# Threshold attention and FFN: a new order of the first blocks, weight sums on TensorE, thresholds on ScalarE

## The chip, the cores and the metric

One core of a Trainium2 chip. The metric is the device time of one execution in microseconds (us), as a median of several runs. A profile is one execution recorded on the chip; its engines are PE (TensorE), PEld (its weight loads), DVE (VectorE), ACT (ScalarE), POOL (GpSimd) and SP (the queue that issues DMAs).

## The reference

```python
# q, k, v: (8 batches, 8 heads, 576 rows, 64); w_in (512, 2048) and w_out (2048, 512) in float64
scores = (q @ k.T) / 8
scores = where(scores >= max(scores) - tau, scores, -1e9)
attn   = exp(scores - max(scores));  attn /= attn.sum() + 1e-9
x      = (attn @ v)  -> (4608 tokens, 512)
out    = maximum(x @ w_in, 0) ** 2 @ w_out
```

## The kernel before

A *block* is 128 rows of queries of a pair of heads; there are 160 of them (the fifth of a pair has 64 rows for each head). A *slot* finishes block n and begins block n+1. A *piece* is 256 tokens of the feed-forward part, which is multiplied with Strassen-like products and so needs sums of weight quarters. The weights come as float64; each of 32 chunks is turned to float32 by a pipeline of *conversion steps* over ScalarE, GpSimd and VectorE:

```python
def weights_step():                 # step m; 36 steps in all
    convert3(m - 4)                 # GpSimd: integer add into w_in / w_out, frees r
    convert1(m - 2)                 # ScalarE: a = |hi|; GpSimd: clip a; ScalarE: r   (2 buffers of r)
    convert2(m - 3)                 # VectorE: shift a, merge into the raw words
    ...                             # fetch the next chunk; make sums due when their chunks are there

def combine_in(n):                  # sums of w_in, on GpSimd, 128x1024 each
    yield plus(e, s1, a21, a22)
    yield minus(e, a21, a11, a21)
    yield minus(e, s2, s1, a11)
    yield minus(e, s4, a12, s2)     # (w_out likewise, half on VectorE)
```

The attention of a block, and the order of a slot:

```python
def softmax(i, t, sc):              # sc: scores in PSUM, two heads
    # VectorE: nmx = -max of each head; thr = -nmx - tau
    # ScalarE: w = exp(sc + nmx), one instruction for each head
    yield
    # VectorE: w = (sc >= thr) * w, with its sum in sm ("the last pass")
    # VectorE: sm += 1e-9; reciprocal;   GpSimd: w *= sm ("normalise")

def slot(n, steps):
    if turns(n): turn(slots[n][0] + 1)             # transpose the next q and k
    begin(n + 1, lambda: weights_due(0))           # scores, softmax; a step between exp and last pass
    values_after(n - 1)                            # attn @ v, copies of x on ScalarE
    ...
    transposes(*slots[n])                          # PE transposes w; ScalarE copies wR, wT, wT
    for k in range(1, steps): weights_due(k)       # a second step, from slot 7 on
```

In the first slots (while weights are converted) every engine runs its instructions in this program order, or nearly so (the trace shows a few of VectorE's swapped from block 8 on). PSUM holds the results of this kernel's matmuls, in banks of 512 float32 columns. In slots 0 to 6 there are two PSUM buffers for scores and two other banks; from slot 7 on one buffer for scores and four other banks. In later slots only PE's order is fixed, and the order on the other engines is the framework's.

## Time and profile before

1628.1 us (1627.2 to 1630.9).

| | before |
|---|---|
| PE busy | 1515.6 us of a span of 1626.5 (93%) |
| DVE, ACT, POOL busy | 867, 586, 592 us |
| row maxima of block 8 / 20 / 26 begin at | 76 / 193 / 245 us |
| PE idle from 245 us on | 37.4 us of 1381.5 |
| PE busy and mean granted clock, 12 to 245 us | 166.5 us of 233, clock 0.81 |

The important reading is by time. Until 245 us PE is idle over a quarter of the time and runs at a lowered clock; after it the kernel is one dense stretch of PE work. So there are two questions for any change: when does the dense stretch start, and how much PE work is left then? The start of a block's row maxima (VectorE's reduction, nmx) is a good mark, as every block has one. Its lines are shown in the prediction.

### The profile page before, as it was taken

The page shows a single profiled execution, that of the slowest core. Times are in us where ns is not written, and L with a number is a line of the kernel's source. Part 1 is how long each engine was busy: PE and PEld are TensorE (multiplying, and loading weights), DVE is VectorE, ACT ScalarE, POOL GpSimd, SP SyncE. Part 2 cuts the span into 40 slices and gives each one's busy share as a digit, 9 for nine tenths or more (in the row PEclk, how much of TensorE's full clock was granted, in tenths as well). Part 3 has the DMA queues.
Part 4 walks back from the last instruction along what each step waited for, and adds up shares of the span by engine and source line. Part 5 has one row for each costly group of instructions (what it writes and reads, how often), then busy time and mean ns, then how long its engine had stood idle before and what let it go on. Part 6 is the DMA issues. An engine that isn't in the chain of part 4 may idle for free.

```text
span 1626.5 us, 25919 instructions
## 1 busy us (share of the span) xinstructions
PE 1515.6 (93%) x10084; PEld 1216.1 (75%) x10084; DVE 867.0 (53%) x1792; ACT 585.7 (36%) x1273; POOL 592.1 (36%) x630
## 2 busy tenths in 40 slices
PE   5676789999999999999999999999999999999998
PEld 2344567778787778778788887878777787878987
DVE  4678974645555564646444455555646464553222
ACT  3545633434343333433333243333433333431100
POOL 2488662332424232334141424232423333233131
PEclk8877889999999999999999999999999999999999
DMA  4334401111010101010101010101011101000000
GB/s 126 109 108 131 128 22 35 23 29 30 23 36 14 31 23 35 23 36 16 35 8 30 21 36 10 34 23 35 23 36 23 35 16 29 15 1 14 14 14 14
DMA packets 107914, 58.69 MB, mean 36 GB/s; under 512 B 89873, under 2 KB 99089, under 8 KB 107793
## 3 DMA queue, kind: packets, MB, share of 16 engines
q1 hardware_dynamic: 107792, 57.04, 12.9%
q8 instruction: 80, 1.31, 0.3%
q14 instruction: 42, 0.34, 0.1%
HBM read 47.58 MB, written 9.44 MB: 35 GB/s over the span
## 4 chain that ended last, share of the span: by engine, by line
PE 77%; DVE 12%; ACT 6%; POOL 3%; issue 2%; SPq 0%; DMA 0%; ACTq 0%; DVEq 0%; POOLq 0%
PE ph L482 27%; PE po L556 25%; PE sc L326 11%; PE pwT L397 6%; DVE nmx L340 5%; ACT w L350 4%; PE pv L428 3%; PE pqk L287 2%; PE pwR L386 2%; DVE s L170 1%; DVE w L355 1%; ACT x L436 1%; PE pv L423 1%; DVE g L491 1%; POOL w L369 1%
## 5 line engine op out<-in xcount | busy, mean ns | idle before, releaser
L369 POOL TENSOR_SCALAR w<-w,sm 128x576 f32<-128x576 f32 (+1 forms) x320 | 237.4, 752 | 643.9 <-DVE sm L360 638.4
L340 DVE TENSOR_REDUCE nmx<-sc 128x1 f32<-128x576 f32 x288 | 206.1, 752 | 206.7 <-PE sc L326 188.9
L355 DVE SCALAR_TENSOR_TENSOR w<-sc,thr,w 128x576 f32<-128x576 f32 x288 | 225.0, 815 | 132.7 <-ACT w L350 130.2
L350 ACT ACTIVATE w<-sc,nmx 128x576 f32<-128x576 f32 x288 | 199.8, 741 | 259.0 <-DVE nmx L340 258.9
L556 PE MATMUL po<-w_out,g 128*128 128x256 f32 x1152 | 261.5, 382 | 11.2 <-ACT x L436 6.1
L556 PEld LDWEIGHTS po<-w_out,g 128*128 128x128 f32 x1152 | 216.1, 191 | 41.0 <-ACT x L436 7.3
L326 PE MATMUL sc<-kT,qT 64*128 64x64 f32 (+3 forms) x1248 | 215.6, 461 | 24.5 <-DVE w L355 24.4
L482 PE MATMUL ph<-x,w_in 128*128 128x128 f32 x1728 | 209.5, 278 | 2.1 <-ACT x L436 2.1
L326 PEld LDWEIGHTS sc<-kT,qT 64*128 64x128 f32 (+1 forms) x1248 | 105.5, 181 | 137.1 <-issue 124.6
L482 PEld LDWEIGHTS ph<-x,w_in 128*128 128x128 f32 x1728 | 203.2, 195 | 3.2 <-ACT x L436 2.3
L397 PE MATMUL pwT<-ident,w 128*128 128x128 f32 x1024 | 146.3, 281 | 44.2 <-ACT x L436 25.7
L397 PEld LDWEIGHTS pwT<-ident,w 128*128 128x128 f32 x1024 | 117.1, 143 | 56.8 <-ACT x L436 37.1
L398 ACT COPY wT<-pwT 128x512 f32<-128x512 f32 x256 | 145.2, 594 | 24.6 <-PE pwT L397 20.8
L482 PE MATMUL ph<-xt,s_in 128*128 128x128 f32 x1152 | 142.4, 278 | 4.3 <-POOL s_in L167 3.3
L428 PE MATMUL pv<-wT,va 128*64 128x320 f32 (+1 forms) x1024 | 141.8, 420 | 0.0
L482 PEld LDWEIGHTS ph<-xt,s_in 128*128 128x128 f32 x1152 | 136.0, 194 | 6.2 <-POOL s_in L167 4.9
L170 DVE TENSOR_TENSOR u<-ph,u 128x512 f32<-128x512 f32 x108 | 74.6, 690 | 112.4 <-PE ph L482 84.2
L556 PE MATMUL po<-t_out,g 128*128 128x256 f32 x576 | 132.2, 379 | 0.0
L428 PEld LDWEIGHTS pv<-wT,va 128*64 128x64 f32 x1024 | 69.4, 140 | 66.5 <-issue 29.9
L556 PEld LDWEIGHTS po<-t_out,g 128*128 128x128 f32 x576 | 107.7, 190 | 13.5
L493 POOL TENSOR_TENSOR g<-p 128x512 f32<-128x512 f32 x36 | 37.8, 1049 | 156.4 <-ACT p L510 156.4
L482 PE MATMUL ph<-x,s_in 128*128 128x128 f32 x576 | 71.9, 279 | 0.0
(79 smaller groups left out, 1623.6 us busy)
## 6 DMA issues: line engine op xcount, KB each, us to landing
kn<-in_k_dram SPq DMA_DIRECT2D x72, 128.0 KB, 3.1
va<-in_v_dram SPq DMA_DIRECT2D x36, 256.0 KB, 2.8
out_dram<-o SPq DMA_DIRECT2D x36, 256.0 KB, 2.0
raw<-in_moe_w_in_dram SPq DMA_DIRECT2D x16, 512.0 KB, 4.0
raw<-in_moe_w_out_dram SPq DMA_DIRECT2D x16, 512.0 KB, 3.8
qn<-in_q_dram SPq DMA_DIRECT2D x56, 128.0 KB, 2.4
rn<-in_q_dram SPq DMA_DIRECT2D x36, 32.0 KB, 2.4
rn<-in_k_dram SPq DMA_DIRECT2D x36, 32.0 KB, 2.7
```

The costliest lines, as they stand in the source:

```text
L170: e.tensor_tensor(out=out, in0=x, in1=y, op=ALU.add)
L326: nc.tensor.matmul(to, qT[rows, ds(t * P, m)], kT[rows, ds(k0, n)], start=True, stop=True)
L340: nc.vector.tensor_reduce(out=nmx[:, j : j + 1], in_=sc[:, ds(at[j], S)], axis=AXIS.X, op=ALU.max, negate=True)
L350: nc.scalar.activation(out=w[:, ts(j, S)], in_=sc[:, ds(at[j], S)], func=AF.Exp, bias=nmx[:, j : j + 1], scale=1.0)
L355: nc.vector.scalar_tensor_tensor(out=w[:, ts(j, S)], in0=sc[:, ds(at[j], S)], scalar=thr[:, j : j + 1], in1=w[:, ts(j, S)], op0=ALU.is_ge, ...
L369: nc.gpsimd.tensor_scalar(out=out, in0=w, scalar1=r, scalar2=1.0, op0=ALU.mult, op1=ALU.mult)
L397: nc.tensor.transpose(pt[:, c, :], w[:, ds(j * (S + REST) + c * P, P)], ident[:, :])
L398: nc.scalar.copy(wT[:, j, :, at], pt[:, :, :])
L428: nc.tensor.matmul(pv[rows, :], va[:, j, c, :], wT[:, j, c, 0:n], start=False, stop=(c == FULL - 1), skip_group_check=True,)
L482: nc.tensor.matmul(to[:, j, :], a, b, start=(not more and j == 0 and c == 0), stop=(c == 1), skip_group_check=True,)
L493: e.tensor_tensor(out=to, in0=c[:, :, :], in1=c[:, :, :], op=ALU.mult)
L556: nc.tensor.matmul(to[:, :], a[:, f, :], b[:, f, :], start=(not more and f == 0), stop=(f == KF - 1), skip_group_check=True,)
```

## The change

Its intent: in the first slots, let PE have its PSUM banks back sooner by copying transposes before the next block's exponentials are through; move the sums from GpSimd to TensorE, which is idle there; relieve VectorE of two small instructions a block.

```diff
+    def combine(out, x, y, sign):            # one PSUM bank, 128x512
+        nc.tensor.matmul(pt, ident, x, start=True, stop=False)
+        nc.tensor.matmul(pt, ident if sign > 0 else nident, y, start=False, stop=True)
+        evicted["n"] += 1                    # then copied out, in turn on ScalarE and VectorE
...                                           # combine_in: 8 sums, twice; combine_out: 16 sums
-        nc.vector.tensor_scalar(out=thr, in0=nmx, scalar1=-1.0, scalar2=tau_p, op0=mult, op1=subtract)
+        nc.scalar.activation(out=thr, in_=nmx, func=AF.Identity, bias=tau_n, scale=-1.0)
+        yield
         for j in range(nj):
             nc.scalar.activation(out=w[j], in_=sc[j], func=AF.Exp, bias=nmx[j], scale=1.0)
-        yield
+            yield
...
-        nc.vector.tensor_scalar(out=sm, in0=sm, scalar1=1e-9, scalar2=None, op0=ALU.add)
+        nc.scalar.activation(out=sm, in_=sm, func=AF.Identity, bias=eps, scale=1.0)
...                                           # transposes() yields after each wT copy
     def slot(n, steps, n_sums):
-            begin(n + 1, lambda: weights_due(0))
+        job = begin(n + 1)                   # scores, row maxima, threshold
...
-        transposes(*slots[n])
-        for k in range(1, steps):
-            weights_due(k)
+        for _ in transposes(*slots[n]):
+            next(job, None)                  # wR, wT, exp, wT, exp
+        for _ in job:
+            pass                             # last pass, epsilon, reciprocal, normalise
+        for k in range(steps):
+            weights_step()
+        for k in range(n_sums):
+            sums_step()                      # 3 a slot
...
-            slot(n, 1)
+            slot(n, 2 - n % 2, 3)            # slots 0 to 6; the early stage ends at slot 25, not 23
```

More of the change, by code (lines that the diff above doesn't have):

```diff
@@ L92 @@
     )
-    tau_p = const.tile([P, 1], FP32, name="tau_p")
-    nc.vector.tensor_scalar(out=tau_p[:, :], in0=tau_c[:, :], scalar1=0.0, scalar2=None, op0=ALU.max)
+    tau_n = const.tile([P, 1], FP32, name="tau_n")
+    nc.vector.tensor_scalar(
+        out=tau_n[:, :], in0=tau_c[:, :], scalar1=0.0, scalar2=-1.0, op0=ALU.max, op1=ALU.mult
+    )
+    eps = const.tile([P, 1], FP32, name="eps")
+    nc.gpsimd.memset(eps[:, :], 1e-9)
+    nident = const.tile([P, P], FP32, name="nident")
+    nc.gpsimd.tensor_scalar(
+        out=nident[:, :], in0=ident[:, :], scalar1=-1.0, scalar2=1.0, op0=ALU.mult, op1=ALU.mult
+    )
     vdiag = [const.tile([P, P], FP32, name=f"vdiag{i}") for i in range(2)]
@@ L170, in plus @@
         e.tensor_tensor(out=out, in0=x, in1=y, op=ALU.add)
+    evicted = {"n": 0}
+    def combine(out, x, y, sign):
+        pt = bank([P, WC], "comb")
+        nc.tensor.matmul(pt[:, :], ident[:, :], x, start=True, stop=False)
+        nc.tensor.matmul(pt[:, :], ident[:, :] if sign > 0 else nident[:, :], y, start=False, stop=True)
+        if len(out.shape) == 3:
+            pt = pt.rearrange("p (f o) -> p f o", f=out.shape[1])
+        evicted["n"] += 1
+        if evicted["n"] % 2:
+            nc.scalar.copy(out, pt)
+        else:
+            nc.vector.tensor_copy(out=out, in_=pt)
@@ L172, in combine_in @@
     def combine_in(n):
-        e = nc.gpsimd
         first, second = ts(n, WC), ds(HF + n * WC, WC)
-        a11, a12 = w_in[:, 0:2, first], w_in[:, 2:4, first]
-        a21, a22 = w_in[:, 0:2, second], w_in[:, 2:4, second]
-        s1, s2, s4 = (s_in[:, m, :, first] for m in range(3))
-        yield plus(e, s1, a21, a22)
-        yield minus(e, a21, a11, a21)
-        yield minus(e, s2, s1, a11)
-        yield minus(e, s4, a12, s2)
-    def combine_out(k):
-        first, second = ds(k, 4), ds(KF + k, 4)
-        b11, b12 = w_out[:, first, 0:HD], w_out[:, first, HD:DM]
-        b21, b22 = w_out[:, second, 0:HD], w_out[:, second, HD:DM]
-        t1, t2, t4 = (t_out[0][:, m, first, :] for m in range(3))
-        minus(nc.vector, t1, b12, b11)
-        yield minus(nc.gpsimd, b12, b22, b12)
-        minus(nc.vector, t2, b22, t1)
-        yield minus(nc.gpsimd, t4, b21, t2)
+        for what in (0, 3, 1, 2):
+            for c in range(2):
+                a11, a12 = w_in[:, c, first], w_in[:, 2 + c, first]
+                a21, a22 = w_in[:, c, second], w_in[:, 2 + c, second]
+                s1, s2, s4 = (s_in[:, m, c, first] for m in range(3))
+                out, x, y, sign = ((s1, a21, a22, 1), (s2, s1, a11, -1), (s4, a12, s2, -1), (a21, a11, a21, -1))[what]
+                combine(out, x, y, sign)
+                yield
@@ new lines, in combine_out @@
+    def combine_out():
+        for what in range(4):
+            for k in range(0, KF, 2):
+                first, second = slice(k, k + 2), slice(KF + k, KF + k + 2)
+                b11, b12 = w_out[:, first, 0:HD], w_out[:, first, HD:DM]
+                b21, b22 = w_out[:, second, 0:HD], w_out[:, second, HD:DM]
+                t1, t2, t4 = (t_out[0][:, m, first, :] for m in range(3))
+                out, x, y = ((t1, b12, b11), (b12, b22, b12), (t2, b22, t1), (t4, b21, t2))[what]
+                combine(out, x, y, -1)
+                yield
@@ L202 @@
     at_step = {"n": 0}
-    sums_due = deque()
+    sums_due, sums_made = deque(), set()
     def weights_step():
@@ L214, in weights_step @@
         if m - 4 in (n_in // 2 - 1, n_in - 1):
-            sums_due.append(combine_in((m - 4) // (n_in // 2)))
+            n = (m - 4) // (n_in // 2)
+            sums_due.append((n, combine_in(n)))
         if m == len(chunks) + 3:
@@ L219, in weights_step @@
             t_out.append(late.tile([P, 3, KF, HD], FP32, name="t_out"))
-            sums_due.extend(combine_out(k) for k in range(0, KF, 4))
+            sums_due.append((2, combine_out()))
     def sums_step():
         while sums_due:
-            if next(sums_due[0], 0) is None:
+            if next(sums_due[0][1], 0) is None:
                 return
-            sums_due.popleft()
+            sums_made.add(sums_due.popleft()[0])
     def weights_until(n):
-        while at_step["n"] < n:
-            weights_step()
-        while at_step["n"] == n and sums_due:
-            sums_step()
+        while n not in sums_made:
+            if sums_due:
+                sums_step()
+            else:
+                weights_step()
     N_STEPS = len(chunks) + 4
@@ L344, in softmax @@
         thr = sb.tile([P, 2], FP32, tag="thr", bufs=3, name="thr")
-        nc.vector.tensor_scalar(
-            out=thr[:, 0:nj], in0=nmx[:, 0:nj], scalar1=-1.0, scalar2=tau_p[:, :], op0=ALU.mult, op1=ALU.subtract
+        nc.scalar.activation(
+            out=thr[:, 0:nj], in_=nmx[:, 0:nj], func=AF.Identity, bias=tau_n[:, :], scale=-1.0
         )
         w = sb.tile([P, 2 * S], FP32, tag="w", bufs=2, name="w")
+        yield
         for j in range(nj):
@@ L352, in softmax @@
             )
-        yield
+            yield
         for j in range(nj):
@@ L358, in softmax @@
             )
-        nc.vector.tensor_scalar(out=sm[:, 0:nj], in0=sm[:, 0:nj], scalar1=1e-9, scalar2=None, op0=ALU.add)
+        nc.scalar.activation(out=sm[:, 0:nj], in_=sm[:, 0:nj], func=AF.Identity, bias=eps[:, :], scale=1.0)
         nc.vector.reciprocal(out=sm[:, 0:nj], in_=sm[:, 0:nj])
@@ L398, in transposes @@
                 nc.scalar.copy(wT[:, j, :, at], pt[:, :, :])
+                yield
         else:
@@ L404, in transposes @@
                 nc.scalar.copy(wT[:, j, :, at], pt[:, :, ds(j * REST, REST)])
+            yield
     def values(i, t0, t1):
@@ L497, in feed_forward @@
         for n in range(2):
-            weights_until(4 + (n + 1) * n_in // 2)
+            weights_until(n)
             X = pm()
@@ L540, in feed_forward @@
         minus(nc.vector, g21, g11, g21)
-        weights_until(N_STEPS)
+        weights_until(2)
         t1, t2, t4 = (t_out[0][:, m, :, :] for m in range(3))
@@ L625, with begin @@
     n_first, n_batch = NP * HALF, NP * NB
-    def begin(n, between=lambda: None):
+    def begin(n):
         i, t = slots[n]
@@ L630, in begin @@
         next(job)
-        between()
-        next(job, None)
+        return job
     def values_after(n):
@@ L651, in turns, with slot @@
         return i + 1 < len(visits) and t == max(visits[i][2] - 2, visits[i][1])
-    def slot(n, steps):
-        def weights_due(k):
-            if k < steps:
-                if at_step["n"] < N_STEPS:
-                    weights_step()
-                sums_step()
+    def slot(n, steps, n_sums):
         if turns(n):
             turn(slots[n][0] + 1)
-        if n + 1 < len(slots):
-            begin(n + 1, lambda: weights_due(0))
+        job = begin(n + 1) if n + 1 < len(slots) else iter(())
         with_values = values_after(n - 1)
@@ L671, in slot @@
             load_v(i + 2)
-        transposes(*slots[n])
-        for k in range(1, steps):
-            weights_due(k)
+        for _ in transposes(*slots[n]):
[3 more added lines that the diff above has]
+        for k in range(steps):
+            if at_step["n"] < N_STEPS:
+                weights_step()
+        for k in range(n_sums):
+            sums_step()
         return with_values
@@ L686 @@
         turn(0)
-        begin(0)
+        for _ in begin(0):
+            pass
         for n in range(n_first - 1):
-            slot(n, 1)
+            slot(n, 2 - n % 2, 3)
     with ExitStack() as stack:
@@ L693 @@
         late = 0.0
-        n_early = n_first - 1 + (N_STEPS + 4 - n_first) // 2
+        n_early = n_first - 1 + (N_STEPS - at_step["n"] + 1) // 2 + 6
         for n in range(n_first - 1, len(slots)):
@@ L698 @@
             with tc.manual_schedule(engines={ET.PE, ET.DVE, ET.Activation, ET.Pool} if early_on else {ET.PE}):
-                with_values = slot(n, 2 if early_on else 1)
+                with_values = slot(n, 2 if early_on else 1, 3)
                 if n < n_first:
```

## The prediction

> **What bounds the kernel now.** I first read the busy time by stretches (columns: stretch, length, busy us and number of instructions of PE, PEld, DVE, ACT and POOL, granted TensorE clock, DMA share, GB/s).
>
> ```profile
> 12.00:70.00 58.00, 38.20 (x162) 21.25 (x162) 32.74 (x78) 27.29 (x58) 21.62 (x31) 0.76 0.38 105
> 70.00:218.00 148.00, 104.84 (x619) 74.67 (x618) 125.41 (x205) 77.12 (x162) 116.06 (x107) 0.82 0.40 112
> 218.00:245.00 27.00, 23.50 (x121) 17.42 (x120) 15.13 (x30) 9.27 (x22) 15.90 (x13) 0.84 0.10 23
> 245.00:1626.50 1381.50, 1344.11 (x9177) 1100.54 (x9173) 692.62 (x1479) 469.89 (x1027) 436.78 (x469) 1.00 0.09 24
> ```
>
> From 245 us on, PE is 97% busy at full clock and every other engine has room: only PE work counts there. What the change can win lies in the first 245 us, where PE is busy 172 us at a clock of 0.76 to 1.0. Busy time times clock is 29.0 + 86.0 + 19.7 = 135 us between 12 and 245, so an estimate of the slack is 233 - 135 = 98 us.
>
> Then the waits of the first 260 us (us in total, times, longest):
>
> ```profile
> ACT w L350 <- DVE nmx L340: 50.1, 18, 8.6
> ACT r L144 <- POOL w_out L164: 24.7, 9, 5.7
> ACT r L144 <- POOL w_in L164: 20.2, 6, 5.6
> PE sc L326 <- DVE w L355: 20.2, 7, 5.3
> PE pwT L397 <- ACT wR L388: 13.9, 4, 3.7
> PE pwT L397 <- ACT x L436: 11.9, 6, 5.7
> ```
>
> PE waits for ScalarE's copies of transposes, which stand behind the next block's exponentials, and for VectorE's last pass over the scores. ScalarE itself waits 45 us in the weight conversion (r), for GpSimd to free one of two r buffers. This wait I expect to decide the matter. The timeline of one two-step block (start, length) shows how it hangs together:
>
> ```profile
> 174.10 0.17 DVE L360 RECIPROCAL sm<-sm 128x2 f32<-128x2 f32 x1
> ...
> 174.43 1.96 POOL L369 TENSOR_SCALAR w<-w,sm 128x576 f32<-128x576 f32 x2 [1.29 <-DVE sm L360]
> 176.36 1.29 POOL L164 TENSOR_TENSOR w_out<-raw,r 128x512 int32<-128x512 int32 x1
> 177.75 0.61 POOL L140 TENSOR_SCALAR a<-a 128x512 f32<-128x512 f32 x1
> 178.32 1.30 POOL L164 TENSOR_TENSOR w_out<-raw,r 128x512 int32<-128x512 int32 x1
> ...
> 177.69 0.68 ACT L144 ACTIVATE r<-raw 128x512 int32<-128x512 uint32 x1 [3.15 <-POOL w_out L164]
> 178.27 1.36 ACT L350 ACTIVATE w<-sc,nmx 128x576 f32<-128x576 f32 x2
> ```
>
> Reciprocal, two normalisations, one integer add on GpSimd, r on ScalarE, then the exponentials: in these early blocks each engine runs in program order, so this is one loop. By the starts of the row maxima (nmx), blocks 1 to 7 begin at 18.4 to 69.7 us, 8.6 us apart (6.7 to 7.0 without a turn of the next q and k, 9.6 to 10 with one). Block 8 begins at 76.4, block 22 at 209.6: 9.5 us each, although two of them stalled on GpSimd's weight sums. Block 26 begins at 245.3, with one piece's hidden half and 48 output matmul instructions done (48 x 216 ns = 10.4 us; 24 of them took 5.18 us in the chain).
>
> **What the Trainium skill says.** "ScalarE: Activation LUTs", What ACT_TABLE_LOAD costs: an ACTIVATE with a per-partition bias costs about 280 ns + 0.833 ns per element. The trace agrees: 0.76 us for 576 elements against 0.741 measured; so a 128x2 threshold is an estimated 0.28 us. "GPSIMD Engine Reference", 8. Key points: it shares SBUF interfaces with VectorE, and contends with its two-port modes. The trace agrees: VectorE's shift (L152) has a median of 0.43 us and takes 1.45 beside GpSimd at 178.46. "PSUM — Partial Sum Buffer", The four PSUM rules: one matmul output is at most one bank, 512 fp32 columns; so each new sum of 128x512 takes one whole bank until it is copied out. No run here shows that yet. "TensorE: Matmul & The Clock Gate", What's actually happening: PE's clock falls when idle and is released by work; agreed, 0.76 to 0.84 before 245 us and 1.00 after.
>
> **The change, part by part.**
>
> *Sums on TensorE.* Removed: 8 GpSimd adds of w_in at 2.35 us (18.8), 4 of w_out (2.36 and 2.87 us, together 10.4), and 4 on VectorE (6.4). Added: 32 sums of 128x512, two fp32 matmuls each. An fp32 matmul is two instructions; a 256-column one takes 216 ns in a dense run, so 512 columns twice is 0.86 us, and 64 matmuls are 55 us of PE at full clock. Also 16 copies on ScalarE (0.59, 9.5 us) and 16 on VectorE (0.69, 11 us). PE is the bound after 245 us, so these 55 us are free only as far as they fill the 98 us of slack. GpSimd's stalls go: row maxima of blocks 10 and 11 lie 18.2 us apart, some 8 us over a usual block; PE waited 104.8 us into the run for s_in.
>
> *Thresholds and epsilon on ScalarE.* VectorE loses two small instructions of 0.17 to 0.23 us a block (0.47 and 0.38 early, under contention); ScalarE gets two of 0.28, one ahead of the exponentials and one between VectorE's last pass and the reciprocal, with two crossings of engines.
>
> *Copies between exponentials.* In program order ScalarE now does threshold, wR copy 0.27, wT 0.59, exp, wT, exp. PE gets its banks earlier, so in the first stage scores need no longer wait for the exponentials. But VectorE's last pass (0.81 each) now waits for later exponentials, and **the conversion steps move behind all of it**: before, the first step lay between the exponentials and that pass, so VectorE converted while ScalarE ran exp.
>
> One two-step block by these durations, from the start of the row maxima: 1.43 both maxima; threshold to 1.8; wR 2.05; wT 2.6; exp 3.3; wT 3.9; exp 4.6; last pass to 5.6; epsilon 5.9; reciprocal 6.1; normalised 7.65; first integer add on GpSimd 8.95; its clip a 9.55; second add 10.85. ScalarE's r: 9.65 and 11.5. VectorE's second conversion needs that clip: 9.7 to 10.9. Only then come the next maxima: **10.9 us a block**. The same loop before is reciprocal 174.1 to reciprocal 182.34: 8.2 us. A one-step block that is followed by a turn: r ends at 9.65, qT 10.15, last transpose 10.4, scores 11.6, rest scores 12.1, next maxima: 12.1 us.
>
> First stage: slots 0 to 6 take 2, 1, 2, 1, 2, 1, 2 steps: 4 x 10.9 + 3 x 12.1 = 79.9, so block 8 begins at 18.4 + 79.9 = 98 us (76.4 before), with 13 of 36 steps done instead of 9. Then 12 slots of two steps: 12 x 10.9 = 131; less 8 for four blocks of a single head half; plus about 18 for hidden-layer adds on VectorE (0.69), turns, and PE waiting for banks in five slots with sums, whose copies stand at the end of ScalarE's and VectorE's order: block 20 at 239. Then 13 sums (22 us) and six slots of about 5.4 us of PE work: 4.0 for attention (1515.6 us of PE busy on the page, less 18 pieces at the code's 48.9 us, over 160 blocks) and 1.44 of hidden layer by the code's quota; at 97%, block 26 at 295. Against 245.3 that is +50, and PE has 10.4 us of output work less behind it: **+60**, so 1689.
>
> **Rivals.**
> *Slack is filled.* If PE ran dense from 12 us on it would need 135 + 55 = 190 us: about 43 us won, 1586. For it: PE's waits for copies and for scores are just those attacked, and GpSimd's bursts vanish. Against: VectorE is already busy 125 of 148 us, the sums use up over half the slack, and the loop above does not run through PE. Half of this (loops of 8 us, sums hidden in gaps) would be 1610 to 1630.
> *The loop is shorter than worked out.* If a buffer comes free earlier, or VectorE without contention (0.43 for 1.45 us) speeds the steps, 1.5 us off each of 19 blocks is -28: 1661.
> *A new wait on the steady path.* Two more ScalarE instructions and crossings lie before scores can be reused in all 160 blocks. For: PE waits there 20.2 us early. Against: after 245 us a block takes some 10 us of PE work, and scores to last pass takes about 7. At most +10 us.
>
> **Range and chances.** The loop's arithmetic gives 1689. Errors of 1 to 2 us in 19 to 25 blocks are 30 to 40 us. I choose a middle of 1682, since the parameters (steps, three sums a slot, six more slots) look tuned and may save something that I do not see. 1640 to 1725 should hold it 8 times in 10. Two per cent is 32.6 us, so slower begins at 1661.5: 0.66. Within 2%: 0.29. Faster would need nearly all the slack: 0.05.
>
> **What would show it.** PE busy about 50 us more in all; from some 300 us on the same 97% at full clock. Row maxima 10 to 12 us apart in blocks 1 to 20, with r still waiting for GpSimd, now behind the normalisation; block 8 near 98 us, block 26 near 295. GpSimd less busy early by 29 us. Fewer PE waits for wR and wT. I am wrong if blocks keep to 8 or 9 us with the steps at their end, or if sums sit in gaps with no later start of the dense part; then the time is about as before or less. If blocks are short but the dense part is less full than 96%, the third rival was underrated.

## The result and the profile after

1706.2 us (1704.2 to 1706.5, 4 runs): slower, ratio 1.047 (95% interval 1.046 to 1.049). A ratio here is the mean time of one kernel's runs over that of the other's in the same rounds, so not quite the ratio of the medians quoted. Executions over 1.5% slower than the fastest of the same kernel are left out of the means.

The stretches of the changed kernel (columns as in the prediction), with the boundary at 327 us, where its block 26 begins:

```profile
12.00:100.00 88.00, 44.90 (x168) 24.38 (x170) 39.11 (x71) 35.00 (x79) 28.43 (x36) 0.67 0.31 88
100.00:250.00 150.00, 111.20 (x504) 66.47 (x501) 81.15 (x133) 71.73 (x157) 68.65 (x73) 0.81 0.32 94
250.00:327.00 77.00, 68.45 (x324) 39.79 (x324) 35.67 (x66) 29.66 (x73) 19.84 (x23) 0.94 0.09 20
327.00:1704.70 1377.70, 1348.13 (x9209) 1106.76 (x9205) 628.12 (x1212) 532.63 (x1297) 448.07 (x475) 1.00 0.09 24
```

Block 26 begins at 327 us instead of 245, 82 us later. All engines are less busy than before in the early stretch: VectorE 120 of the 238 us from 12 to 250, where it was busy 173 of the 233 from 12 to 245. So nothing is overloaded; the engines wait for each other. Busy time times clock up to 327 us is 30.1 + 90.1 + 64.3 = 185 us: 50 us more PE work done than in the kernel before at its block 26, and 130 us of slack where there were 98. By then 8 output matmul instructions were done instead of 48, which leaves some 9 us more for later. And the dense stretch has 29.6 us of PE idle where it had 37.4. 82 + 9 - 8 = 83, against a difference of spans of 78; the account is good to some 5 us, since the busy time of matmuls is modelled.

The waits of the first 300 us of the changed kernel:

```profile
POOL w L397 <- DVE sm L388: 159.3, 23, 10.6
DVE w L383 <- ACT w L378: 69.7, 22, 6.7
...
ACT sm L387 <- DVE w L383: 31.6, 22, 1.7
ACT r L152 <- POOL w_in L172: 30.6, 15, 3.0
ACT r L152 <- POOL w_out L172: 25.3, 14, 3.0
...
PE pwR L414 <- POOL w L397: 17.1, 7, 4.8
...
PE sc L353 <- DVE w L383: 12.8, 5, 5.9
```

And one line of the same view of before, for its first 260 us:

```profile
DVE w L355 <- ACT w L350: 8.5, 14, 1.4
```

PE's waits for the last pass did go down (20.2 to 12.8 us), but VectorE now waits 70 us for exponentials (8.5 before), and r still waits for GpSimd, 56 us instead of 45. One two-step block in order of time, put together from the rows of its engines in the timeline:

```profile
51.83 0.17 DVE L388 RECIPROCAL sm<-sm 128x2 f32<-128x2 f32 x1 [0.36 <-ACT sm L387]
...
52.19 1.91 POOL L397 TENSOR_SCALAR w<-w,sm 128x576 f32<-128x576 f32 x2 [9.80 <-DVE sm L388]
...
54.06 1.29 POOL L172 TENSOR_TENSOR w_in<-raw,r 128x512 int32<-128x512 int32 x1
...
55.38 0.67 ACT L152 ACTIVATE r<-raw 128x512 int32<-128x512 uint32 x1 [3.03 <-POOL w_in L172]
...
56.15 1.45 DVE L160 TENSOR_SCALAR raw<-a 128x512 int32<-128x512 int32 x1 [2.66 <-ACT r L152]
...
57.34 0.67 ACT L152 ACTIVATE r<-raw 128x512 int32<-128x512 uint32 x1 [0.73 <-POOL w_in L172]
...
58.53 1.41 DVE L367 TENSOR_REDUCE nmx<-sc 128x1 f32<-128x576 f32 x2
...
59.97 0.29 ACT L372 ACTIVATE thr<-nmx,tau_n 128x2 f32<-128x2 f32 x1 [1.96 <-DVE nmx L367]
```

This is the loop of the prediction: the next maxima start 6.7 us after the reciprocal, behind normalisation, add, r and VectorE's second conversion. What the prediction had not seen lies in front of the same block:

```profile
43.92 0.30 ACT L372 ACTIVATE thr<-nmx,tau_n 128x2 f32<-128x2 f32 x1 [2.11 <-DVE nmx L367]
46.35 0.37 ACT L466 COPY x<-pv 128x256 f32<-128x256 f32 x1 [2.14 <-PE pv L458]
...
49.90 0.82 DVE L383 SCALAR_TENSOR_TENSOR w<-sc,thr,w 128x576 f32<-128x576 f32 x1 [6.02 <-ACT w L378]
```

When a block's values are due, ScalarE's copy of x now stands between threshold and exponentials, and PE makes the product it copies only after the scores. Here it held the exponentials 2.1 us and VectorE was idle 6.0 us. In the kernel before, the exponentials came first; these are rows of ScalarE in the same block (row maxima at 36.08 us):

```profile
37.62 1.37 ACT L350 ACTIVATE w<-sc,nmx 128x576 f32<-128x576 f32 x2 [3.37 <-DVE nmx L340]
...
39.43 0.66 ACT L144 ACTIVATE r<-raw 128x512 int32<-128x512 uint32 x1
39.98 0.37 ACT L436 COPY x<-pv 128x256 f32<-128x256 f32 x1
```

### The profile page after: what moved, and what is told of

It reads as the page before. It is cut to its first block, busy times and chain, and to the rows that moved or that the text cites. A ratio compares the mean times of both kernels' runs of the same rounds, so it can differ in the third digit from the quotient of the medians.

```text
span 1704.7 us, 26129 instructions
## 1 busy us (share of the span) xinstructions
PE 1577.6 (93%) x10212; PEld 1239.6 (73%) x10212; DVE 785.1 (46%) x1484; ACT 671.2 (39%) x1609; POOL 567.0 (33%) x620
## 3 DMA queue, kind: packets, MB, share of 16 engines
q1 hardware_dynamic: 107792, 57.04, 12.1%
## 4 chain that ended last, share of the span: by engine, by line
PE 80%; DVE 10%; ACT 5%; POOL 3%; issue 1%; DMA 0%; SPq 0%; DVEq 0%; POOLq 0%; ACTq 0%
PE ph L512 26%; PE po L586 23%; PE sc L353 10%; PE pwT L425 6%; PE pv L458 6%; DVE nmx L367 2%; PE pv L453 2%; PE pwR L414 2%; ACT w L378 2%; PE pqk L314 2%; DVE w L383 2%; DVE s L178 2%; DVE g L175 1%; POOL w L397 1%; PE comb L185 1%
## 5 line engine op out<-in xcount | busy, mean ns | idle before, releaser
L397 POOL TENSOR_SCALAR w<-w,sm 128x576 f32<-128x576 f32 (+1 forms) x320 | 244.0, 772 | 796.9 <-DVE sm L388 793.9
L378 ACT ACTIVATE w<-sc,nmx 128x576 f32<-128x576 f32 x288 | 203.4, 738 | 0.0
L425 PE MATMUL pwT<-ident,w 128*128 128x128 f32 x1024 | 147.4, 285 | 38.5 <-ACT x L466 22.6
L425 PEld LDWEIGHTS pwT<-ident,w 128*128 128x128 f32 x1024 | 120.6, 146 | 48.8 <-ACT x L466 26.6
L372 ACT ACTIVATE thr<-nmx,tau_n 128x2 f32<-128x2 f32 (+1 forms) x160 | 47.6, 298 | 235.4 <-DVE nmx L367 233.8
L387 ACT ACTIVATE sm<-sm,eps 128x2 f32<-128x2 f32 (+1 forms) x160 | 47.3, 296 | 143.4 <-DVE w L383 143.4
```

What stands on the lines that cost most here:

```text
L372: nc.scalar.activation(out=thr[:, 0:nj], in_=nmx[:, 0:nj], func=AF.Identity, bias=tau_n[:, :], scale=-1.0)
L378: nc.scalar.activation(out=w[:, ts(j, S)], in_=sc[:, ds(at[j], S)], func=AF.Exp, bias=nmx[:, j : j + 1], scale=1.0)
L397: nc.gpsimd.tensor_scalar(out=out, in0=w, scalar1=r, scalar2=1.0, op0=ALU.mult, op1=ALU.mult)
L425: nc.tensor.transpose(pt[:, c, :], w[:, ds(j * (S + REST) + c * P, P)], ident[:, :])
```

## Experiments

Two theories. **A, the loop**: conversion steps and copies now stand in one chain with the exponentials, and this chain makes the early blocks longer; the sums fill part of the slack. **B, the PE work**: the 55 us of new PE work are the loss. Twelve kernels were run, each correct. Times are medians beside the kernel before on the same chip (1628.5 to 1628.7). The intervals of the ratios are 0.1 to 0.2% either way; b_thr, b_altmid and the four hyb kernels differ from before by less than 2%, which the record counts as the same, and b_sums and a_mid lie too near 2% to be placed, so what is said of them rests on these intervals. The last three columns are the start of the row maxima.

| kernel | us | ratio to before | block 8 | block 20 | block 26 |
|---|---|---|---|---|---|
| before | 1628 | | 76 | 193 | 245 |
| changed | 1706 | 1.047 | 108 | 267 | 327 |
| b_sums | 1660 | 1.019 | 76 | 197 | 261 |
| b_thr | 1648 | 1.012 | 88 | 204 | 262 |
| b_alt | 1679 | 1.031 | 91 | 230 | 296 |
| a_nosums | 1684 | 1.034 | 115 | 252 | 305 |
| b_altmid | 1659 | 1.019 | 83 | 209 | 269 |
| b_alt_r3 | 1669 | 1.025 | 81 | 218 | 283 |
| a_thr | 1699 | 1.043 | 107 | 253 | 309 |
| a_mid | 1663 | 1.021 | 91 | 223 | 283 |
| hyb | 1618 | 0.994 | 77 | 192 | 243 |
| hyb_r3 | 1616 | 0.992 | 77 | 191 | 243 |
| hyb_o | 1627 | 0.999 | 77 | 191 | 244 |
| hyb_t | 1632 | 1.002 | 76 | 192 | 243 |

### The three parts alone, and the change without its sums

**b_sums**: the kernel before, with `combine` as in the diff and three sums at a slot's end. It also takes the diff's formula for the end of the early stage, which gives slot 27 here instead of 23.

> The kernel before with the weight sums alone moved to TensorE (32 sums of two matmuls, 3 a slot, copies in turn on ScalarE and VectorE; conversion steps, exponentials and thresholds as before). Theory A (the longer loop through the conversion steps makes most of the loss, and sums partly fill PE's gaps): 1640 to 1665 us, and row maxima of block 20 no later than 200 us (193 before). Theory B (the 55 us of new PE work are the loss, the loop hides): 1680 us or more, with PE's slack before the dense part unchanged at some 98 us.

1660.0 us. Blocks are as early as before until block 8, and block 20 is at 197; the dense stretch starts 15 us later. Theory A's size. The 55 us of PE work cost 31, so by subtraction the slack took 24 of them. The stretches agree: busy time times clock from 12 us to block 26 is 176 us of 249, a slack of 72 us where before has 98. (No output matmul instruction is done by then, where before has 48. What the longer early stage does alone was not run.) That GpSimd's stall is gone bought nothing visible: block 11 begins at 114 us (111 before). In the changed kernel the sums also hold up the new order. Four rows of its timeline:

```profile
110.48 2.08 PE L186 MATMUL comb<-w_in,ident 128*128 128x512 f32 x2 [2.49 <-POOL w_in L172]
113.62 2.07 PE L185 MATMUL comb<-w_in,ident 128*128 128x512 f32 x2 [1.07 <-ACT s_in L191]
...
117.43 0.58 ACT L191 COPY w_in<-comb 128x512 f32<-128x512 f32 x1 [3.68 <-PE comb L186]
118.44 0.27 ACT L416 COPY wR<-pwR 128x128 f32<-128x128 f32 x1 [0.42 <-PE pwR L414]
```

PE waits for a chunk that GpSimd has just added, then for a bank that ScalarE has yet to copy, and runs the sum at half its pace (2.08 us where the same pair takes 1.02 later in that stretch); ScalarE waits 3.7 us for the third sum before it gets to copies and exponentials. Row maxima of blocks 8 and 9 lie 22.6 us apart there.

**b_thr**: `thr` and `sm + 1e-9` as in the diff, nothing else.

> The kernel before with thresholds and epsilon alone on ScalarE. Theories A and B: within 0.7% of before, 1617 to 1640 us, as PE is the bound after 245 us and VectorE gains about what ScalarE loses before. The third rival of the prediction (a new wait on the steady path) expects 1638 us or more, with PE's waits for the last pass over the scores up.

1648.3 us: outside the range of both theories, and the size that the third rival gave, but not in its place. PE idle between 350 and 1500 us is 28.7 us (27.0 before); 12 of the 20 us are lost in the first blocks, where block 8 begins at 88 us instead of 76. PE's waits for the last pass did go up as that rival said, from 20.2 to 31.4 us in the first 260 us. The timeline shows why; this is the block whose rows of before are shown above (row maxima here at 40.38 us):

```profile
43.90 0.67 ACT L148 ACTIVATE r<-raw 128x512 int32<-128x512 uint32 x1
45.08 0.30 ACT L363 ACTIVATE sm<-sm,eps 128x2 f32<-128x2 f32 x1 [0.52 <-DVE w L359]
45.29 0.35 ACT L440 COPY x<-pv 128x256 f32<-128x256 f32 x1
```

In program order the epsilon instruction stands ahead of the copies of x and wR. It must wait for VectorE's last pass, so ScalarE, which before went straight on to its copies, waits too, and PE behind it for banks. The copy of x begins 4.9 us after the row maxima here and 3.9 us after them before. In each of blocks 1 to 8 ScalarE's first copy comes 0.9 to 1.0 us later in this way: 0.1 to 0.2 us of it is the threshold ahead of the exponentials, the rest the epsilon and its wait. So it was mostly 0.3 us of work that put the last pass into a chain it had not been in; no run moves the epsilon or the threshold alone.

**b_alt**: the order of the diff alone; step counts of before (1, then 2), all steps at the slot's end.

> The kernel before with the new order alone: copies of transposes between the exponentials, conversion steps (same counts, 1 then 2 a slot) behind the last pass at the slot's end; sums still on GpSimd and VectorE, thresholds on VectorE. Theory A: 1655 to 1690 us; row maxima in two-step slots 10 to 12 us apart instead of 7 to 9.5. Theory B: 1640 us or less.

1679.4 us, as theory A has it, and from block 8 to block 20 the row maxima lie 11.6 us apart in the mean (9.8 before). This is the largest of the three parts.

**a_nosums**: the changed kernel with `combine_in`, `combine_out` and their places as before.

> The changed kernel with the weight sums back on GpSimd and VectorE (all else as changed). Theory A: 1655 to 1690 us, so that the sums are worth 15 to 50 us and the order the rest. Theory B: 1650 us or less, as the 55 us of PE work are gone. PE busy falls by about 55 us of 1578 in both.

1684.3 us. Theory B falls: without the PE work (busy 1516 us, not 1578) the changed kernel is still 55 us slower than before, and its block 26 is at 305. The sums are worth 22 us on top of the rest and 31 alone. The parts overlap: alone they cost 31 + 20 + 51 = 102 us, together 78. Two more changes of the diff, the step counts of slots 0 to 6 and the end of the early stage, never ran alone; what they cost is not known.

### What in the order costs

**b_altmid**: b_alt, with one move.

```diff
+        for k in range(steps):
+            if k == 1: (last pass, reciprocal, normalise)
+            weights_step(); sums_step()      # the first step now ahead of the last pass
```

> b_alt (the new order on the kernel before, 1679 us) with the first conversion step of a slot moved back between the exponentials and VectorE's last pass. Theory A (the place of the conversion steps makes the longer loop): 1630 to 1655 us, two thirds or more of the 51 us come back. Rival C (the copies of transposes and of x ahead of the exponentials make it, whatever the steps do): 1668 us or more.

1659.0 us: 20 of the 51 us come back, less than theory A's two thirds, more than rival C allows. Both hold in part: the place of the first step is 20 us. The other 30 are what is left of the order, that is the copies of wR, wT and x ahead of the exponentials (the second step is at the slot's end, where it was before). VectorE's waits fit that: in the first 260 us it still waits 48.7 us for exponentials, as in b_alt (47.6), against 8.5 before.

**b_alt_r3**: b_alt with `r` in three buffers.

```diff
-        r = conv.tile([P, WC], I32, tag="r", bufs=2, name="r")
+        r = conv.tile([P, WC], I32, tag="r", bufs=3, name="r")
```

> b_alt with three r buffers instead of two, so that ScalarE's r waits for an integer add of GpSimd one step older, in one-step slots one that is long done. If ScalarE's wait for the r buffer closes the loop, as the prediction put it: 1665 us or less (two us or more off each one-step slot, one to two off each two-step slot). If VectorE's second conversion closes it, which waits for GpSimd's clip behind the same normalisation whatever r does: 1670 to 1681 us.

1668.5 us: 11 us back, between the two ranges, though ScalarE's waits for r fell from 87 to 19 us in the first 260 us. The wait for the r buffer is on the loop, mostly in the first stage (block 8 at 81 instead of 91), but it is a fifth of the cost of the order, not what decides it.

**a_mid**: the changed kernel, with the first step moved ahead of the last pass as in b_altmid.

> The changed kernel with one thing undone: the first conversion step of a slot stands again between the exponentials and VectorE's last pass. On the kernel before this was worth 20 us (b_alt 1679 to b_altmid 1659). If the place of the steps costs as much in the whole change: 1676 to 1692 us. If thresholds on ScalarE and the sums' copies set the pace in its stead: 1697 us or more.

1663.3 us: one move takes back 43 of the 78 us, more than either range had and twice what it gave in b_alt. A block of its timeline:

```profile
59.95 1.42 DVE L367 TENSOR_REDUCE nmx<-sc 128x1 f32<-128x576 f32 x2 [2.87 <-PE sc L357]
61.29 0.42 DVE L160 TENSOR_SCALAR raw<-a 128x512 int32<-128x512 int32 x1
61.74 0.69 DVE L164 SCALAR_TENSOR_TENSOR raw<-raw 128x512 int32<-128x512 int32 x1
...
66.47 0.82 DVE L383 SCALAR_TENSOR_TENSOR w<-sc,thr,w 128x576 f32<-128x576 f32 x1 [4.04 <-ACT w L378]
```

VectorE converts (0.42 and 0.69 us) in the time in which it would wait for the exponentials anyway, and beside an idle GpSimd. The slot's other conversion then takes 0.43 and 1.11 us at 68.48 us, so no shift of this slot takes 1.45 us as above. The maxima of the next block need no longer wait for this step. Why the move is worth twice as much here as in b_alt was not traced.

**a_thr**: the changed kernel with thresholds and epsilon on VectorE.

> The changed kernel with thresholds and epsilon back on VectorE. b_thr cost 20 us on the kernel before, most of it before 250 us. If that cost adds to the others: 1686 to 1696 us. If the other waits of the changed order hide it: 1700 us or more. The dense part should lose the some 8 us that it gained in the changed kernel (PE idle 27 us between 350 and 1500 us in the kernel before, 19 in the changed one), if thresholds on ScalarE are needed for that gain.

1699.1 us: 7 us back, of the 20 that this part costs alone; it falls just short of the second range, so most of it is hidden by the other waits. PE idle between 350 and 1500 us is 23.5 us, up from 18.7.

### A version that beats both

In the dense stretch the changed kernel is better. Stretches of before, changed and hyb:

```profile
350.00:1500.00 1150.00, 1122.97 (x7720) 910.62 (x7719) 605.91 (x1304) 416.02 (x913) 372.99 (x410) 1.00 0.10 25
```

```profile
350.00:1500.00 1150.00, 1131.27 (x7823) 917.55 (x7821) 558.41 (x1099) 489.55 (x1200) 379.03 (x415) 1.00 0.10 27
```

```profile
350.00:1500.00 1150.00, 1127.78 (x7765) 917.84 (x7764) 543.47 (x1061) 473.18 (x1156) 380.86 (x412) 1.00 0.09 25
```

PE idle is 27.0, 18.7 and 22.2 us. **hyb** keeps the early slots of before and takes from the end of the early stage (slot 23) the changed order and thresholds; sums stay on GpSimd and VectorE:

```diff
-                with_values = slot(n, 2 if early_on else 1)
+                with_values = slot(n, 2 if early_on else 1, not early_on)   # last argument: order and thr/eps as changed
```

> The kernel before in its early slots, and from the dense part on the changed order with thresholds and epsilon on ScalarE; sums on GpSimd. If the 8 us less of PE idle in the dense part belong to that order: 1618 to 1624 us. If they come from the later start and other pacing of the changed kernel: 1626 to 1632 us, the same as before.

1617.8 us (5 rounds), ratio 0.994 (0.992 to 0.995) to the kernel before: faster by 11 us. Some 5 us of it are the idle above; by block 26 it is 2 us ahead. Over the whole span the other 6 us are PE busy time: the same 10084 instructions took 1509.7 us instead of 1515.6. Why they did I did not trace.

**hyb_o** has only the changed order in the dense stretch (thresholds on VectorE everywhere), **hyb_t** only the thresholds there (order of before).

> hyb with the changed order alone in the dense part, thresholds and epsilon on VectorE everywhere. If the 11 us need both parts, as a_thr and b_thr suggest (PE idle of 23.5 and 28.7 us between 350 and 1500 us, against 18.7 with both): 1622 to 1630 us.

> hyb with thresholds and epsilon alone on ScalarE in the dense part, in the order of before. If both parts are needed: 1622 to 1630 us; if ScalarE's thresholds alone do it: 1615 to 1621 us.

1627.5 us (ratio 0.999) and 1631.9 us (1.002, some 2 us above its first range): either part alone is worth nothing or costs a little; only both together gain. PE's idle time agrees: from 350 to 1500 us it is 27.1 and 28.2 us in these two, 18.7 to 22.2 us in each of the five kernels that have both parts there, and 23.5 to 28.7 us in each of the nine that lack one. Why they need each other is open: in this stretch the order on ScalarE and VectorE is the framework's, so a changed program changes more than the lines that were edited.

**hyb_r3** adds the third r buffer.

> hyb (1618 us: order of before in the early slots, changed order and thresholds from the dense part on) with three r buffers. ScalarE waits 45 us early for an r buffer in the kernel before; in b_alt a third buffer gave 11 us. If the wait lies on the loop here too: 1603 to 1613 us. If VectorE, busy 125 of 148 us there, sets the pace: 1614 to 1619 us.

1615.8 us, ratio 0.992 (0.991 to 0.994): the third buffer gives at most 2 us here, which overlaps hyb's interval. The waits for r went from 45 to 2 us in the first 260 us, and block 26 hardly moved. In the order of before, these waits do not lie on the chain that sets the blocks' pace.

## Why the prediction was right, and where its sizes were off

- *Slower, 1682 us, range 1640 to 1725*: measured 1706, in the range, and 24 us above its middle. I had lowered the middle below the sum of the steps (1689) because the parameters looked tuned. No run supports that; the sum was nearer. That it missed by only 17 us is partly luck: it had block 26 at 295 us, and block 26 came 32 us later than that; 8 us less PE idle in the dense stretch, which nobody expected, and some 5 us that the account above does not close made up for part. (The border of slower, 1661.5 in the text, should be 1660.7; nothing hangs on it.)
- *Only work and slack before the dense stretch count*: held. The ends differ by what block 26 and the work left there say, to some 5 us.
- *55 us of PE work for 64 matmuls, free as far as they fill slack*: held. PE ran 128 more instructions and was 62 us busier; b_sums puts what the slack took at 24 us, its stretches at 26.
- *The loop, 10.9 us for a two-step block and 12.1 for a one-step block with a turn*: the second was measured at 11.85 three times. The first was 16.1 and 15.8 (and from block 7 to block 8 10.5 to the first maximum, 14.6 to the second); only slot 0 took 10.1, and its two steps hold no integer add yet. **This is the term that was too small**: I let ScalarE go from the threshold straight to wR and forgot that the copy of x, with PE's product before it, stands in between in every later two-step slot of the first stage (shown above: exponentials 2.1 us later, VectorE idle 6.0 us). Of the 5.2 us that the block shown took too long, 3.4 had been lost by the reciprocal; 0.6 went to the normalisation and 1.2 to VectorE's second conversion, which took 2.4 us beside GpSimd's add where I had 1.2.
- *About 18 us for adds, turns and bank waits in slots with sums*: also too small. Blocks 8 to 9 took 22.6 us and blocks 12 to 13 took 24 us; from block 8 to block 20 the sum had 141 us and the run took 159. Block 8 was put at 98 and block 20 at 239; they came at 108 and 267. Block 26 was put at 295 and came at 327.
- *"This wait I expect to decide the matter" (r for GpSimd)*: only in part. A third r buffer took back 11 of 51 us. The place of the first step, the bold point of the prediction's third part, was worth 20 us in b_alt and 43 in the whole change. What the copies ahead of the exponentials cost, 30 us by b_altmid, I had counted in the loop but not named.
- *Rival "slack is filled"*: fell. Slack grew from 98 to 130 us. *Rival "a new wait on the steady path", at most 10 us*: wrong in place and size. b_thr cost 20 us, most of it in the first blocks, and mostly through the epsilon's place in ScalarE's order. *Row "97% in the dense part as before"*: PE idle fell by 8 us; I had expected none.
- *The figure of "ScalarE: Activation LUTs", What ACT_TABLE_LOAD costs*: held. It gave an estimate of 0.28 us for the 128x2 threshold; the median measured is 0.296.
- *A small slip*: not every early interval without a turn is 6.7 to 7.0 us; that from block 1 to block 2 is 8.1. Nothing rests on it.

## What to carry to other kernels

When engines run in program order, ask for each instruction not only how long it takes but what it waits for and what stands behind it: a 0.3 us instruction that waits for another engine made its whole queue wait some 0.8 us a block, and together with the threshold cost 20 us. Filler work (here, conversions) belongs where its engine would wait anyway; moved to the end of the loop, it becomes part of the loop (moving one step back was worth 20 and 43 us here). And an order that is better in one stage can be tried there alone: the changed order lost in the early stage and won, with thresholds on ScalarE, in the dense one.

## What the Trainium skill lacked or had wrong

- "GPSIMD Engine Reference", 8. Key points, says that GpSimd contends with VectorE's two-port modes; that list gives no size (another page of the skill treats who waits for how long, so a reference is what is missing). Here VectorE's 128x512 shift took 1.45 us beside GpSimd work and 0.42 to 0.43 alone, and a pair of GpSimd's normalisations took 1.91 to 1.93 us beside VectorE's conversion and 1.47 us in a block without it.
- "TensorE: Matmul & The Clock Gate", Back-to-back issue gap, gives N/2.4 + 2.5 ns for an isolated matmul; that section does not say what changes for float32 (another page does, so again a reference is missing). By its formula a 256-column instruction takes an estimated 109 ns; here 24 float32 ones in a dense run took 5.18 us, 216 ns each, and each float32 matmul was two such instructions.
- No page that I looked up warns that a tiny instruction in an in-order engine's queue can cost far more than its duration through what it waits for: 0.3 us for each epsilon, some 0.8 us of delay with its wait in each of blocks 1 to 8, 20 us in b_thr together with the thresholds.
